# Loading every fourth streamed weight piece with two transfers, of 120 and of 8 partitions

## The chip, the cores and the metric

The kernel runs on one core of one Trainium2 chip. The metric is the device time of one execution in microseconds (us); lower is better. Where two kernels are compared, the ratio is the mean time of the fast runs of one kernel over the mean time of the fast runs of the other in the same rounds, so it is not quite the ratio of the medians that are quoted.

## The reference, cut to what matters

A recurrent attention over 64 segments of 32 tokens, with 8 memory tokens that each segment hands to the next, is mixed by a gate with a gated feed-forward network of the same input.

```python
mem = mem0
for s in range(n_seg):                       # 64, one after the other: mem is the carry
    h = concatenate([mem, x[:, 32*s:32*s+32]])
    q = einsum('btd,dhe->bhte', h, Wq)       # Dm = 640, H = 32, Dh = 192
    k = einsum('btd,dhe->bhte', h, Wk)
    v = einsum('btd,dhe->bhte', h, Wv)
    p = softmax(where(mask, q @ k.T * scale, -1e9))
    o = einsum('bhte,hed->btd', p @ v, Wo)
    mem = o[:, :8]
    outs.append(o[:, 8:])
a = concatenate(outs)
b = (gelu(x @ w_gate) * (x @ w_up)) @ w_down
return g * a + (1 - g) * b                   # g = sigmoid(sum(x * gate_w))
```

The four attention weights are needed again in each of the 64 segments. They don't all fit into on-chip memory, so a part is resident and the rest is streamed anew for each segment.

## The kernel before

The weights are cut into pieces. A piece of Wq, Wk or Wv is 128 partitions of 3,072 bytes (384 KB); a piece of Wo is 128 partitions of two rows of 1,280 bytes (320 KB). In each segment 24 pieces are streamed, 15 of the first kind and 9 of the second, through a ring of five slots. SyncE issues the loads. Before each it waits until PE has used up the piece that had the slot.

```python
B_RING = int(opts.get("ring", 5))
r_ring = [sreg(o, GQ) for o in ring_off]
...
def piece_src(key):
    if key[0] == 3:
        return Wo2[:, 2 * key[1]:2 * key[1] + 2, :]
    m, o_, k = key
    return (Wq2, Wk2, Wv2)[m][:, k, OW * o_:OW * (o_ + 1)]
...
def issue_ring(seg, upto):
    done = issued.get(seg, 0)
    while done <= upto:
        key = order[stream_list[done]]
        slot = stream_counter[0] % B_RING
        S_.add("sp", lambda e, slot=slot, key=key: e.dma_start(piece_view(key, ring_off[slot]), piece_src(key)),
               writes=[r_ring[slot]], dma_sem="ring%d" % slot, name="ring s%d p%d" % (seg, done))
        stream_counter[0] += 1
        ring_of[(seg, key)] = slot
        done += 1
    issued[seg] = done
```

Per four segments, `perm_dma` loads 128 rows of x, loads 128 rows of the feed-forward result and stores 128 rows of output, each as two transfers whose memory side is a view of four groups of rows:

```python
def rows(ap, g):
    v = ap[128 * g:128 * g + 128, :].rearrange("(s t) d -> s t d", t=L)
    return v[:, 0:XA, :], v[:, XA:L, :]      # four times 24 rows, four times 8 rows
```

## Time and profile before

| what | number | from |
|---|---|---|
| time | 2167.59 us median of 3 (2164.26 to 2174.91) | runs |
| loop of 64 segments | from about 330 us on, 28.6 us each | trace |
| PE busy in the loop | 85% | windows |
| DMA in the loop | 96% busy, 322 GB/s | windows |
| PE waiting for the four weights | 158 us | waits |
| median 3,072-byte packet | 121 ns (mean 141) | packets |

The page's own view of the transfers: busy tenths and rate in 40 slices of the span, then packets by queue.

```profile
DMA  9203579999999999999999999999999999999998
GB/s 366 103 13 89 149 220 341 328 321 337 322 325 316 310 326 329 313 327 311 329 328 314 324 315 332 323 307 316 334 319 333 320 325 306 328 327 328 322 321 273
...
q1 hardware_dynamic: 311914, 601.41, 81.6%
...
q8 instruction: 315, 5.16, 0.9%
```

From slice 7 on, the last slice apart, the sixteen DMA engines are busy at least 90% of the time. Queue 1 is SyncE's, with the weights. Queue 8 holds 315 packets of 16 KB. PE has two times 40,326 = 80,652 instructions, which is 315 blocks of 256 to within one block, so these are PE's instruction fetches.

The chain of work that ended last, by engine and by line:

```profile
DMA 48%; PE 37%; DVE 9%; ACTq 3%; issue 2%; ACT 2%; SPq 0%; POOL 0%; DVEq 0%; POOLq 0%
DMA arena<-in_A_Wq_dram 19%; DMA arena<-in_A_Wo_dram 13%; DMA arena<-in_A_Wv_dram 10%; PE ps L872 9%; PE ps L1021 7%; PE ps L899 5%; DMA arena<-in_A_Wk_dram 4%; PE ps L804 3%; PE ps L742 2%; ACTq L819 2%; PE ps L739 2%; PE ps L757 2%; PE ps L992 2%; DVE arena L975 2%; DVE arena L1008 1%
```

Waits of PE, longest in total first (us, times, longest one), and the issues of the ring (count, KB, median us from issue to landing):

```profile
PE ps L872 <- DMA arena<-in_A_Wq_dram: 77.6, 127, 1.9
...
PE ps L899 <- DMA arena<-in_A_Wv_dram: 32.2, 50, 1.8
PE ps L1021 <- DMA arena<-in_A_Wo_dram: 30.6, 63, 3.0
...
PE ps L872 <- DMA arena<-in_A_Wk_dram: 12.3, 16, 1.5
```

```profile
arena<-in_A_Wo_dram SPq DMA_DIRECT2D x591, 320.0 KB, 4.9
arena<-in_A_Wq_dram SPq DMA_DIRECT2D x404, 384.0 KB, 5.3
arena<-in_A_Wv_dram SPq DMA_DIRECT2D x335, 384.0 KB, 5.1
```

And the middle of the loop, from 600 to 1800 us (window, its length, busy us and instructions of PE, PE's weight loads, DVE, ACT, POOL, then granted clock, DMA share, GB/s):

```profile
600.00:1800.00 1200.00, 1016.72 (x25314) 668.11 (x25318) 747.97 (x2482) 353.79 (x885) 174.56 (x773) 0.98 0.96 322
```

Half of the chain is flights of weight pieces, and PE's largest waits are for them. So what makes a piece land earlier or later is worth time here.

### The profile page before, as it was taken

How to read it: one execution, taken by the hardware profiler on the slowest of the kernel's cores; microseconds unless marked ns; L12 is line 12 of the kernel's file. 1: busy time of each engine (PE TensorE's matmuls, PEld its weight loads, DVE VectorE, ACT ScalarE, POOL GpSimd, SP SyncE). 2: the span in 40 equal slices, each digit the busy share in tenths (PEclk: the TensorE clock that was granted, in tenths of full speed). 3: DMA queues.
4: the chain of work that ended last, by engine and by line, in shares of the span. 5: the costliest groups of instructions: out<-in, count | busy, mean ns of one | idle time of the engine just before them, and what ended most of it. 6: DMA issues, size and time to landing. Idle time of an engine off the chain costs nothing.

```text
span 2166.5 us, 92005 instructions
## 1 busy us (share of the span) xinstructions
PE 1836.7 (85%) x40326; PEld 1154.9 (53%) x40326; DVE 1231.5 (57%) x3952; ACT 618.8 (29%) x1480; POOL 274.1 (13%) x1210
## 2 busy tenths in 40 slices
PE   7999948888888888888888888888888888888887
PEld 3544425555555555555555555555555555555555
DVE  2222316666656566656666666656666666666665
ACT  2222212333232223332322223322323222323232
POOL 0000001111111111111111111111111111111111
PEclk9999979999999999999999999999999999999999
DMA  9203579999999999999999999999999999999998
GB/s 366 103 13 89 149 220 341 328 321 337 322 325 316 310 326 329 313 327 311 329 328 314 324 315 332 323 307 316 334 319 333 320 325 306 328 327 328 322 321 273
DMA packets 363391, 642.97 MB, mean 297 GB/s; under 512 B 60514, under 2 KB 231786, under 8 KB 362986
## 3 DMA queue, kind: packets, MB, share of 16 engines
q1 hardware_dynamic: 311914, 601.41, 81.6%
q10 hardware_dynamic: 51072, 35.66, 5.7%
q8 instruction: 315, 5.16, 0.9%
q14 instruction: 90, 0.74, 0.1%
HBM read 619.13 MB, written 17.83 MB: 294 GB/s over the span
## 4 chain that ended last, share of the span: by engine, by line
DMA 48%; PE 37%; DVE 9%; ACTq 3%; issue 2%; ACT 2%; SPq 0%; POOL 0%; DVEq 0%; POOLq 0%
DMA arena<-in_A_Wq_dram 19%; DMA arena<-in_A_Wo_dram 13%; DMA arena<-in_A_Wv_dram 10%; PE ps L872 9%; PE ps L1021 7%; PE ps L899 5%; DMA arena<-in_A_Wk_dram 4%; PE ps L804 3%; PE ps L742 2%; ACTq L819 2%; PE ps L739 2%; PE ps L757 2%; PE ps L992 2%; DVE arena L975 2%; DVE arena L1008 1%
## 5 line engine op out<-in xcount | busy, mean ns | idle before, releaser
L872 PE MATMUL ps<-arena 128*32 128x384 bf16 x10240 | 566.8, 331 | 119.9 <-DMA arena<-in_A_Wq_dram 77.6
L1021 PE MATMUL ps<-arena 128*128 128x40 bf16 x15360 | 472.1, 181 | 71.7 <-DVE arena L1008 35.9
L1021 PEld LDWEIGHTS ps<-arena 128*128 128x128 bf16 x15360 | 434.9, 97 | 116.8 <-DVE arena L1008 48.0
L872 PEld LDWEIGHTS ps<-arena 128*32 128x32 bf16 x10240 | 239.6, 96 | 346.5 <-DMA arena<-in_A_Wq_dram 172.1
L876 ACT ACTIVATE arena<-ps 128x384 bf16<-128x384 f32 x512 | 251.4, 491 | 552.2 <-PE ps L872 446.8
L899 PE MATMUL ps<-arena 128*32 128x384 bf16 x6400 | 333.1, 331 | 37.0 <-DMA arena<-in_A_Wv_dram 32.2
L835 POOL COPY arena<-arena 128x96 bf16<-128x96 bf16 x256 | 67.6, 264 | 1645.1 <-PE ps L931 1089.0
L899 PEld LDWEIGHTS ps<-arena 128*32 128x32 bf16 x6400 | 150.5, 97 | 175.6 <-DMA arena<-in_A_Wv_dram 82.0
L882 DVE STREAM_TRANSPOSE arena<-arena 128x384 bf16<-128x384 bf16 x256 | 146.0, 570 | 102.3 <-ACT arena L876 102.3
L975 DVE TENSOR_TENSOR arena<-ps,arena 128x320 bf16<-128x320 bf16 x256 | 125.8, 491 | 125.9 <-PE ps L973 121.9
L1002 ACT ACTIVATE arena<-ps 128x320 bf16<-128x320 f32 x256 | 110.7, 432 | 229.4 <-PE ps L994 229.4
L910 ACT ACTIVATE arena<-ps 128x384 bf16<-128x384 f32 x256 | 125.6, 491 | 161.9 <-PE ps L899 161.9
L839 POOL COPY arena<-arena 64x32 bf16<-64x32 bf16 (+1 forms) x768 | 165.7, 216 | 47.3
L959 DVE TENSOR_REDUCE arena<-ps 104x4 f32<-104x160 f32 x256 | 82.6, 323 | 150.6 <-ACT ps L957 148.6
L992 PE MATMUL ps<-arena 128*128 128x160 bf16 (+1 forms) x768 | 133.7, 264 | 39.6 <-DVE arena L978 38.0
L889 DVE STREAM_TRANSPOSE arena<-arena 64x128 bf16<-64x128 bf16 x512 | 145.5, 284 | 8.1
L957 ACT ACTIVATE ps<-ps 104x160 f32<-104x160 f32 x256 | 74.0, 289 | 233.9 <-DVE ps L947 189.0
L994 PE MATMUL ps<-arena 128*128 128x64 bf16 (+1 forms) x768 | 128.0, 206 | 2.1 <-DMA arena<-in_A_Wv_dram 1.0
L945 DVE TENSOR_REDUCE arena<-ps 104x4 f32<-104x160 f32 x256 | 81.0, 316 | 77.0 <-PE ps L931 77.0
L885 DVE STREAM_TRANSPOSE arena<-arena 128x256 bf16<-128x256 bf16 x256 | 111.4, 435 | 16.1 <-ACT arena L876 16.1
L992 PEld LDWEIGHTS ps<-arena 128*128 128x128 bf16 x768 | 73.9, 99 | 85.5 <-DVE arena L978 60.3
L1006 DVE CAST arena<-ps 64x160 bf16<-64x160 f32 x256 | 80.4, 314 | 52.5 <-PE ps L994 48.4
(79 smaller groups left out, 1719.8 us busy)
## 6 DMA issues: line engine op xcount, KB each, us to landing
arena<-in_A_Wo_dram SPq DMA_DIRECT2D x591, 320.0 KB, 4.9
arena<-in_A_Wq_dram SPq DMA_DIRECT2D x404, 384.0 KB, 5.3
arena<-in_A_Wv_dram SPq DMA_DIRECT2D x335, 384.0 KB, 5.1
arena<-in_A_Wk_dram SPq DMA_DIRECT2D x276, 384.0 KB, 5.3
left_qk_scratch<-arena ACTq DMA_DIRECT2D x16, 768.0 KB, 8.8
arena<-left_qk_scratch ACTq DMA_DIRECT2D x64, 192.0 KB, 4.5
arena<-in_A_x_dram SPq DMA_DIRECT2D x4, 640.0 KB, 15.1
ffn_b_scratch<-arena ACTq DMA_DIRECT2D x16, 160.0 KB, 1.8
```

The costliest lines, as they stand in the source:

```text
L839: S_.add("pool", lambda e, a=a, b=b, lo=lo, hi=hi, sa=sa: e.tensor_copy(out=Ks[lo:hi, a:b, L:R], in_=stg[lo:hi, o, 1, sa:sa + b - a]), rea ...
L872: S_.add("pe", [lambda e, j=j, k=k, gv=gv: e.matmul(ps[32 * j:32 * j + 32, bank, 0:384].rearrange("p (c i) -> p c i", i=32), Hb[hb][:, k, ...
L876: S_.add("act", lambda e: e.activation(out=rows_sb[m], in_=ps[:, bank, 0:384], func=ACTF.Copy), reads=[r_ps[bank]], writes=[r_rows[m]], na ...
L882: S_.add("dve", lambda e: e.transpose(out=Qs[:, :, 0:L], in_=rows_sb[0].rearrange("p (c r) -> p c r", r=L)), reads=[r_rows[0]], writes=[r_ ...
L885: S_.add("dve", lambda e: e.transpose(out=apx(Ks[:, 0, :], [[2 * R, 4], [R, 2], [1, L]]), in_=apx(rows_sb[1], [[96, 4], [64, 2], [1, L]])) ...
L889: S_.add("dve", lambda e, a=a, lo=lo: e.transpose(out=Ks[lo:lo + 64, a:a + 4, 0:L], in_=src[lo:lo + 64, :, 1]), reads=[r_rows[1]], writes= ...
L899: return [lambda e, j=j: e.matmul(ps[32 * j:32 * j + 32, bk, 0:384], lhs, g_[:, 384 * j:384 * (j + 1)], start=(k == 0), stop=(k == KT - 1) ...
L910: S_.add("act", lambda e: e.activation(out=v_sb[o % NVB], in_=ps[:, bank, 0:384], func=ACTF.Copy), reads=[r_ps[bank]], writes=[r_v[o % NVB ...
L975: S_.add("dve", lambda e: e.tensor_tensor(out=PTm, in0=apx(pv[:, 512:616], [[64, 2], [0, 4], [1, R]]), in1=apx(mbd, [[0, 2], [1, 4], [0, R]]),
L992: return [lambda e: e.matmul(full, v[:, e0:e0 + 128], PTm[:, ia:ib], start=True, stop=False, skip_group_check=True), lambda e: e.matmul(pa ...
L994: lambda e: e.matmul(part, vl[:, e0:e0 + 128], PTl[:, ia:ib], start=False, stop=True, skip_group_check=True)]
L1021: fns.append(lambda e, g_=g_, i=i, c=c, n=n, tl=tl, cc=cc, u=u: e.matmul(ps[:, OB, n * R:(n + 1) * R], g_[:, i, n * 128:(n + 1) * 128], u[ ...
```

## The change

The intent rests on an assumption: that a transfer of 120 partitions leaves out one of the DMA engines, the one that has extra work (here, the instruction fetches). Then a piece in four that passes it by could let it catch up. The eight partitions left over go in a small second transfer.

```diff
+    r_rings = [(sreg(o, GQ, 0, 120), sreg(o, GQ, 120, 128)) for o in ring_off]
...
-            S_.add("sp", lambda e, slot=slot, key=key: e.dma_start(piece_view(key, ring_off[slot]), piece_src(key)),
-                   writes=[r_ring[slot]], dma_sem="ring%d" % slot, name="ring s%d p%d" % (seg, done))
+            cut = 120 if done % 4 == 1 else 128
+            for lo, hi in ((0, cut), (cut, 128)):
+                if lo < hi:
+                    S_.add("sp", lambda e, slot=slot, key=key, lo=lo, hi=hi: e.dma_start(
+                        piece_view(key, ring_off[slot])[lo:hi], piece_src(key)[lo:hi]),
+                        writes=[r_ring[slot] if cut == 128 else r_rings[slot][lo > 0]], dma_sem="ring%d%s" % (slot, "t" if lo else ""),
+                        name="ring s%d p%d" % (seg, done))
```

## The prediction

> **What bounds the kernel now.** From about 330 us the kernel runs 64 segments of about 28.6 us. There the windows table gives PE 85% busy, DMA engines 96% and 322 GB/s; the chain of waits is 48% DMA, nearly all ring pieces (24 a segment: 15 of 384 KB, 9 of 320 KB), 37% PE. The waits view has PE idle about 157 us for the four weights.
>
> One DMA engine is the laggard. The sixteen semaphore landings of a ring transfer lie evenly, except the last: for 384 KB medians are 3.15 us (first), 4.59 (15th), 5.17 (16th) after issue. Queue 8 explains it: 315 packets of 16 KB, exactly 80,652 PE instructions in blocks of 256; they never overlap each other and take 0.96 us about every 6 us, 17% of one engine's time.[...] Estimate from packet times (121 ns per 3,072 B, 55 per 1,280 B): a segment costs each engine about 22.5 us, this one 27 of 28.6.
>
> **Which engine?** The trace does not number engines. [...]loads of 8 and 5 partitions and of 4-row views show 9, 6 and 5 semaphore writes[...].[...] I take it to be the last, at about 0.8.
>
> **What changes.** Pieces 1, 5, 9, 13, 17, 21 of each segment (four of 384 KB, two of 320 KB) go as 120 partitions[...] plus 8[...].[...] SyncE issues 6 more transfers a segment (0.33 to 0.40 us each; it mostly waits). PE waits on one more semaphore for these. Bytes and arithmetic stay.
>
> **Worth.** Had each 16th landing come with its 15th, 127 of 167 us of PE's ring waits would go, at first order; along the chain, 177 ring flights carry 146 us of that gap. Not all is had: the next engine is close, fetches still delay momentarily,[...] the tail is issued 0.35 us later, PE, once faster, asks sooner, and waits for DVE stay. I expect half: about 65 us (3%).
>
> **Predicted: 2105 us, 2050 to 2165 with 8 in 10.** Faster by over 2%: 0.60; within 2%: 0.31; slower: 0.09.
>
> **What would show it.** Right: the 16th landing within 0.3 us of the 15th, median landing 4.6 to 4.9 us; PE's waits for weights 60 to 110 us; loop bandwidth 330 to 340 GB/s at unchanged bytes; less DMA in the chain; queue 8 unchanged. Wrong on the engine: the last gap unchanged[...] or larger[...]. Wrong on size: gap gone but PE waits barely smaller.
>
> **What would make it wrong.** The fetch engine is not the last;[...] transfers run less evenly; the tail, queued behind other work, becomes the new last landing; SyncE's extra issues delay bursts.

The forecast came to about 65 us gained: half of the 127 to 146 us that the last landings cost by the trace, the half being a guess. Terms, namely what each engine gains and loses in a segment, rested on which engines a transfer uses, which no trace shows, and are not in the 65 us as numbers. "The last" engine is a name from that same assumption.

## The result, and the profile after

| | before | after |
|---|---|---|
| time, median of 4 | 2165.93 us (2161.73 to 2174.91) | 2461.09 us (2449.19 to 2476.15) |
| ratio of the fast runs | | 1.134, 95% interval 1.128 to 1.140 |

The prediction was 2105 us; the kernel became 13% slower instead. Each of the 384 cut pieces (6 x 64) costs (2461.09 - 2165.93) / 384 = 0.77 us.

The transfers of the changed kernel, by slices and queue:

```profile
DMA  9105699999999999999999999999999999999998
GB/s 371 43 23 136 185 283 270 279 278 283 281 273 276 283 271 280 273 289 276 276 272 280 279 279 281 267 280 276 293 277 283 277 292 279 268 278 284 279 274 239
...
q1 hardware_dynamic: 314602, 601.42, 85.6%
...
q8 instruction: 315, 5.16, 1.0%
```

Its chain by engine, PE's waits, and ring issues, as above:

```profile
DMA 64%; PE 27%; DVE 4%; ACTq 3%; issue 1%; ACT 1%; SPq 0%; POOL 0%; DVEq 0%
```

```profile
PE ps L878 <- DMA arena<-in_A_Wq_dram: 102.3, 179, 2.7
PE ps L878 <- DMA arena<-in_A_Wk_dram: 79.7, 149, 1.7
PE ps L1027 <- DMA arena<-in_A_Wo_dram: 79.2, 169, 2.0
PE ps L905 <- DMA arena<-in_A_Wv_dram: 63.1, 89, 2.6
PE ps L1000 <- DMA arena<-in_A_Wv_dram: 46.1, 79, 2.7
```

```profile
arena<-in_A_Wq_dram SPq DMA_DIRECT2D x404, 384.0 KB, 6.0
...
arena<-in_A_Wv_dram SPq DMA_DIRECT2D x192, 360.0 KB, 6.7
arena<-in_A_Wv_dram SPq DMA_DIRECT2D x143, 384.0 KB, 6.0
```

```profile
600.00:1800.00 1200.00, 933.70 (x21927) 598.54 (x21919) 650.41 (x2158) 307.56 (x768) 150.22 (x666) 0.96 0.99 278
```

Bytes and fetches are the same (601 MB, 315). The engines are busier than before (0.99) and move less: 278 GB/s against 322. An engine that is busy and moves less has slower packets, and that is what the packet records of the loop show (computed from the trace's packets of queue 1, from 330 to 2150 us):

| 3,072-byte packets in the loop | before | after |
|---|---|---|
| mean / median | 141 / 121 ns | 170 / 151 ns |
| share at the floor (at most 124 ns) | 87% | 31% |

The fetch packets became slower too (mean 1.01 to 1.19 us). PE's granted clock was a little lower (0.96 against 0.98) and its busy time longer (1836.7 to 1926.4 us), but its share of the chain fell from 37 to 27%, and the streams below are slow with PE idle, so this is not the main cause. The uncut pieces are hit as well: Wq is cut nowhere, yet its pieces land after 6.0 us instead of 5.3. So the question is not what the second transfer costs, but why most packets take longer, those of the uncut pieces too.

The semaphore writes: in the loop a 120-partition load shows 16, the first of them 0.54 us after the issue (median of 326 loads; the second at 3.72 us), and its tail shows 9, as the one load of 8 partitions in the kernel before. In an uncut 384 KB piece of the kernel before the first of the 16 comes after 3.15 us. How many engines that makes, no trace shows.

### The profile page after: what moved, and what is told of

Same layout as the page of the kernel before. It is cut to its first block, busy times and chain, and to the rows that moved or that the text cites. A ratio compares the mean times of both kernels' runs of the same rounds, so it can differ in the third digit from the quotient of the medians.

```text
span 2457.5 us, 92505 instructions
## 1 busy us (share of the span) xinstructions
PE 1926.4 (78%) x40298; PEld 1189.3 (48%) x40326; DVE 1232.7 (50%) x3952; ACT 620.0 (25%) x1480; POOL 273.6 (11%) x1210
## 4 chain that ended last, share of the span: by engine, by line
DMA 64%; PE 27%; DVE 4%; ACTq 3%; issue 1%; ACT 1%; SPq 0%; POOL 0%; DVEq 0%
DMA arena<-in_A_Wo_dram 21%; DMA arena<-in_A_Wq_dram 17%; DMA arena<-in_A_Wv_dram 15%; DMA arena<-in_A_Wk_dram 10%; PE ps L1027 5%; PE ps L878 5%; PE ps L905 5%; PE ps L810 3%; PE ps L748 2%; ACTq L825 2%; PE ps L745 2%; PE ps L763 2%; DVE arena L981 1%; PE ps L998 1%; DMA arena<-in_B_w_up_dram 1%
## 5 line engine op out<-in xcount | busy, mean ns | idle before, releaser
L878 PE MATMUL ps<-arena 128*32 128x384 bf16 x10240 | 614.9, 338 | 206.1 <-DMA arena<-in_A_Wq_dram 102.3
L1027 PE MATMUL ps<-arena 128*128 128x40 bf16 x15360 | 496.8, 182 | 111.2 <-DMA arena<-in_A_Wo_dram 79.2
L1027 PEld LDWEIGHTS ps<-arena 128*128 128x128 bf16 x15360 | 449.6, 98 | 167.5 <-DMA arena<-in_A_Wo_dram 104.2
L878 PEld LDWEIGHTS ps<-arena 128*32 128x32 bf16 x10240 | 243.3, 97 | 466.5 <-DMA arena<-in_A_Wq_dram 193.6
L905 PE MATMUL ps<-arena 128*32 128x384 bf16 x6400 | 349.7, 334 | 78.7 <-DMA arena<-in_A_Wv_dram 63.1
L905 PEld LDWEIGHTS ps<-arena 128*32 128x32 bf16 x6400 | 167.2, 97 | 211.3 <-DMA arena<-in_A_Wv_dram 107.2
L1000 PE MATMUL ps<-arena 128*128 128x64 bf16 (+1 forms) x768 | 133.2, 209 | 47.8 <-DMA arena<-in_A_Wv_dram 46.1
L998 PEld LDWEIGHTS ps<-arena 128*128 128x128 bf16 x768 | 75.2, 101 | 74.7 <-DVE arena L984 41.8
L1000 PEld LDWEIGHTS ps<-arena 128*128 128x128 bf16 x768 | 76.9, 100 | 68.6 <-DMA arena<-in_A_Wv_dram 68.0
```

The source lines that it names most:

```text
L878: S_.add("pe", [lambda e, j=j, k=k, gv=gv: e.matmul(ps[32 * j:32 * j + 32, bank, 0:384].rearrange("p (c i) -> p c i", i=32), Hb[hb][:, k, ...
L905: return [lambda e, j=j: e.matmul(ps[32 * j:32 * j + 32, bk, 0:384], lhs, g_[:, 384 * j:384 * (j + 1)], start=(k == 0), stop=(k == KT - 1) ...
L998: return [lambda e: e.matmul(full, v[:, e0:e0 + 128], PTm[:, ia:ib], start=True, stop=False, skip_group_check=True), lambda e: e.matmul(pa ...
L1000: lambda e: e.matmul(part, vl[:, e0:e0 + 128], PTl[:, ia:ib], start=False, stop=True, skip_group_check=True)]
L1027: fns.append(lambda e, g_=g_, i=i, c=c, n=n, tl=tl, cc=cc, u=u: e.matmul(ps[:, OB, n * R:(n + 1) * R], g_[:, i, n * 128:(n + 1) * 128], u[ ...
```

## The experiments

My theory formed after the result: packets take longer because of where a transfer of another shape writes, and the number of partitions tells which shapes are slow. The grounds that I gave for it, in terms of engines and of the memory they write, no trace shows. Where a text names no theory, the first numbers are those that this one led me to expect.

The rivals: the second transfer and its semaphore; unequal work of the engines; the tail of eight partitions; the order in which memory rows are read.

Where only a number at the end of a kernel was wanted, loads were added after the last output; they don't touch the result.

### Lone loads

```diff
     out_store(NG - 1)
+    r_mic = sreg(0, ring_bytes)
+    def lone(n, dst, src):
+        for rep in range(3):                 # each waits for the one before: same region
+            S_.add("sp", lambda e: dst(e, src), writes=[r_mic], dma_sem="mic%d" % n, watch=True)
+    lone(0, lambda e, s: e.dma_start(sb(slice(0, 128)), s), hb(0, 128))    # Wq rows, 4 x 3,072 bytes each
+    lone(1, lambda e, s: e.dma_start(sb(slice(0, 120)), s), hb(0, 120))
     ...
+    lone(5, lambda e, s: e.dma_start(sb(slice(120, 128)), s), hb(120, 128))
+    lone(7, lambda e, s: e.dma_start(sb(slice(0, 32, 4)), s), hb(120, 128))
```

> The kernel before, with 42 lone loads at its very end (14 shapes, three times each, each issued after the one before has landed; rows of 3,072 bytes, four per partition). [...]a packet takes about 121 ns in the 128-partition load, but about twice that (230 to 250 ns) in the loads of 120, 112, 64 and 60 partitions and of 32[...], and about four times (450 to 490 ns) in 8 partitions in[...]; back to about 121 ns[...] for 8 partitions in steps of four[...]. Rival, transfer count and engine balance (each transfer costs a fixed time, the packets don't care where they go): about 121 ns in all of them, times set by packets per engine alone. Rival, memory side (rows read in a bad order): the 8 rows with destinations in steps of four stay as slow as the 8 rows to neighbours. The kernel itself unchanged, longer only by the loads at the end (some 150 to 250 us).

(The loads "in a row" went to the eight neighbouring partitions 120 to 127.) After that I put the pattern into a rule, before the second set. No trace shows what it counts, and it had to set the load of 128 partitions apart.

> Lone loads at the end again, twelve other shapes, three times each. The first lone loads (120: 241 ns a packet, 64: 234, 60: 236, 112: 175, against 121 in 128)[...]. The rule therefore expects a median packet of 121 ns for 128, 126, 117 and 117 from partition 2, about 240 for 120, 230 to 245 or (as 112) 175 to 240 for 105, 104 and 96, 240 to 360 for 45. 15 partitions in steps of nine: from first packet to landing 1.0 to 1.4 us; 15 neighbours, the same rows: about 1 us longer. The rival,[...] a number of partitions that is not a multiple of 16 is slow as such[...]: 126 and 117 stretched like 120.

Measured in both (packets of 3,072 bytes, three loads of each shape; the whole of it at a time when nothing else ran):

| partitions | median packet, ns | landing after issue, us |
|---|---|---|
| 128 | 121 | 6.4 to 6.8 |
| 126 | 121 | 6.9 to 7.3 |
| 117 | 121 | 6.7 to 7.6 |
| 120 | 239 to 245 | 9.6 to 10.0 |
| 104 | 239 to 244 | 9.4 to 9.5 |
| 64 | 230 to 235 | 6.0 to 6.3 |
| 60 | 235 to 237 | 5.9 to 6.2 |
| 96 | 195 to 208 | 7.4 to 7.5 |
| 112 | 172 to 182 | 7.3 to 7.5 |
| 105 | 145 to 167 | 6.7 to 7.3 |
| 45 | 271 to 303 | 5.8 to 5.9 |
| 32 | 130 to 151 (mean 212 to 215) | 3.9 to 4.1 |

Issues of the second set on SyncE's queue (start, time from the first of three issues to the end of the third, line, count). L1095 is 128 partitions, L1096 126, L1097 120, L1098 117, L1101 104:

```profile
2167.99 13.61 SPq L1095 DMA_DIRECT2D arena<-in_A_Wq_dram  x3
2188.08 14.67 SPq L1096 DMA_DIRECT2D arena<-in_A_Wq_dram  x3
2209.32 20.01 SPq L1097 DMA_DIRECT2D arena<-in_A_Wq_dram  x3
2238.58 13.83 SPq L1098 DMA_DIRECT2D arena<-in_A_Wq_dram  x3
...
2301.54 19.26 SPq L1101 DMA_DIRECT2D arena<-in_A_Wq_dram  x3
```

Each of these times holds two landings and one issue. 120 partitions take about 1.4 times as long as 126 (20.01 against 14.67 us), although they are fewer. A 120-partition load alone has packets of about twice the floor (239 to 245 against 121 ns). A number that isn't a multiple of 16 is not slow as such: 126 and 117 stay at the floor (121 ns), while 112, 96 and 64 don't (172 to 235 ns). The rule's expectation for the second set told the fast shapes (126 and 117) from the slow ones (120, 105, 104, 96, 45), with 105 less slow than expected (145 to 167 against 175 to 245 ns). Why these shapes differ is not shown.

Two pairs that read the same rows into other partitions speak against the memory side. Time from the first packet to the landing: rows 120 to 127 into eight neighbouring partitions, 2.2 to 2.3 us; the same rows into partitions 0, 4, ... 28, 1.1 to 1.2 us. Fifteen rows into neighbours, 2.4 us; the same into partitions 0, 9, ... 126, 1.3 to 1.4 us. From issue to landing they differ by less (3.1 to 3.2 against 2.6 to 2.7, and 3.3 to 3.4 against 2.9 to 3.1), because the first packet of the stepped loads comes later (1.5 to 1.7 us after the issue against about 0.9, by difference). There the packets themselves end early in either case (median 121 to 123 ns), and into neighbours the landing comes 1.0 to 1.3 us after the last packet's end, against 0.3. Why is not shown. For the large shapes the memory side was not tested by a pair of its own. My expectation of 450 ns for these packets was wrong, and so was that of 230 to 250 ns for 32 partitions. Three shapes of the first set missed their aim: memory views of 8 or 2 groups were to change the engines in use, but the semaphore writes (16 and 9) are as many as without them, so those three say nothing.

### Two transfers, but of columns

```diff
+            cut = done % 4 == 1
+            for n in range(2 if cut else 1):
                 ... half(piece_view(key, ring_off[slot]), key, n) ... half(piece_src(key), key, n)
```

> The same pieces in two transfers, but cut along the columns: both halves have 128 partitions[...]. [...]within 2% of the kernel before (2165 us), packets at their floor. Rival, two transfers and a second semaphore cost the time: slower by several per cent, up to the 13% of the change.

Measured: 2197.51 us against 2169.59, ratio 1.014 (1.009 to 1.019). 3,072-byte packets stay at a mean of 141 ns. So as many second transfers, issues and semaphores as in the change, all of 128 partitions, cost 1.4%; the smaller packets of the halved rows may be part of it (not separated). The middle of the loop stays near that of the kernel before:

```profile
600.00:1800.00 1200.00, 1013.99 (x25111) 665.40 (x25113) 746.79 (x2479) 352.65 (x881) 174.47 (x768) 0.99 0.95 319
```

### The same pieces as 112 and 16 partitions

```diff
+            parts = [(0, 112), (112, 128)] if done % 4 == 1 else [(0, 128)]
```

> The same pieces cut into 112 and 16 partitions[...]. [...]clearly slower, by 7 to 15%, with stretched packets (mean of 3,072-byte packets 155 to 175 ns against 141). Rival, engine balance[...]: as before within 2%.

Measured: 2388.58 us, ratio 1.102 (1.097 to 1.106); mean packet 164 ns (141 before). I took every engine to have as many packets here as before; no trace shows that, so this speaks against unequal work as the main cause only if it holds. The middle of the loop:

```profile
600.00:1800.00 1200.00, 961.37 (x22704) 617.41 (x22704) 674.78 (x2237) 317.23 (x793) 157.04 (x691) 0.96 0.99 288
```

### Main part without the tail

```diff
+            parts = [(0, 120)] if done % 4 == 1 else [(0, 128)]     # 120..127 keep an older piece: wrong on purpose
```

> Only the 120-partition part of the cut pieces is loaded, the last 8 partitions keep an older piece (a wrong result on purpose). It tells main part from tail. If the main part is the cost: still 7 to 13% slower than before. If the tail[...] is the cost: near the time before or faster, 2080 to 2170 us[...]. If both: between, 4 to 8% slower.

Measured: 2416.01 us, ratio 1.114 (1.109 to 1.118), result wrong. So about 11 of the 13% come with the large part, and about two with the tail (roughly, since this kernel also moves 1.5% fewer weight bytes, 592 MB).

### 126 and 2 partitions

Alone, the packets of 126 partitions were as short as those of 128. If what makes a lone load slow were the whole story, this cut would repair the change. (The rival here: any cut along the partitions is slow.)

```diff
+            parts = [(0, 126), (126, 128)] if done % 4 == 1 else [(0, 128)]     # and with done % 8 == 1
```

> The change with another cut: 126 and 2 partitions instead of 120 and 8, every fourth piece. [...]most of the loss goes: 2110 to 2230 us, at most 3% slower than before and at least 9% faster than the change; if relieving the fetch engine is worth what was predicted, up to 3% faster than before. Rival[...]: 10% or more slower than before.

> The same with every eighth piece cut (three in a segment). [...]between before and every fourth, 2110 to 2200 us[...]. Rival: 5% or more slower.

Measured: every fourth piece, 2436.56 us, ratio 1.124 (1.120 to 1.127), mean packet 166 ns; every eighth, 2274.81 us, ratio 1.052 (1.046 to 1.058). Both expectations were missed, the first by 9% even from its upper end (2230 us): the theory was not complete. The middle of the loop with 126 and 2 looks like that of the change:

```profile
600.00:1800.00 1200.00, 938.61 (x22117) 602.86 (x22117) 658.64 (x2182) 310.50 (x774) 152.52 (x672) 0.95 0.98 280
```

### The change at a third of the dose

```diff
+            parts = [(0, 120), (120, 128)] if done % 12 == 5 else [(0, 128)]
```

> The change itself (120 and 8) at a third of the dose: two pieces in a segment. If each cut piece costs the same (0.76 us, 292 us over 384 cut pieces), 3.5 to 6% slower than before, 2245 to 2295 us. If a few cut pieces suffice[...], nearly as slow as the change. If relief pays at a small dose, within 2%.

Measured: 2265.27 us, ratio 1.045 (1.041 to 1.049): (2265.27 - 2164.64) / 128 = 0.79 us for each cut piece, as in the full change. For this cut the cost is proportional to the number of cut pieces at the two doses tried, and no gain shows at the small one. For 126 and 2 it is less so: 0.71 us for each cut piece at every fourth, 0.57 at every eighth.

### Streams, as in the ring

What differs between a lone load and the loop is that other pieces are in flight. So pieces of one shape, and of two shapes mixed, were sent as in the ring, without the loop.

```diff
+    def stream(n, parts):
+        for j in range(20):                  # five slots in flight
+            P = parts[j % len(parts)]
+            S_.add("sp", lambda e, j=j, P=P: e.dma_start(arena[0:P, (j % 5) * OW:(j % 5 + 1) * OW], Wq2[0:P, j % KT, 0:OW]),
+                   writes=[r_ring[j % 5]], dma_sem="mic%d_%d" % (n, j % 5), watch=True)
+    stream(0, [128]); stream(1, [126]); stream(2, [128, 126]); stream(3, [120])
+    stream(4, [128, 120]); stream(5, [128, 128, 128, 120]); stream(6, [128, 128, 128, 126]); stream(7, [128])
```

> The kernel before with eight streams of 20 ring loads at its end (3,072 bytes a partition, five in flight, as in the loop): all 128 partitions; all 126; 128 and 126 by turns; all 120; 128 and 120 by turns; three of 128 and one of 120; three of 128 and one of 126; all 128 again. The cut of 126 was as slow in the loop as that of 120, though alone it was not. Theory A[...]. Expected: all 128: packets 121 ns in median, 300 to 340 GB/s; all 126 between; 128 and 126 by turns stretched (mean over 155 ns, rate at least 8% under all 128), three to one less so, 120 slowest (180 to 220 GB/s). Theory B (126 is slow in the loop only for the tail of two partitions or for the loop's waits): the streams of 126 and the mixed ones at the floor like 128.

The eight streams in this order, each from its first issue to its last landing; the last two numbers are DMA share and GB/s (the first stream overlaps the end of the kernel):

```profile
2161.40:2185.30 23.90, 0.45 (x5) 0.28 (x5) 1.61 (x4) 0.00 (x0) 0.00 (x0) 0.54 0.91 336
2188.50:2217.60 29.10, 0.00 (x0) 0.00 (x0) 0.00 (x0) 0.00 (x0) 0.00 (x0) 0.50 0.84 266
2220.70:2251.30 30.60, 0.00 (x0) 0.00 (x0) 0.00 (x0) 0.00 (x0) 0.00 (x0) 0.50 0.90 255
2254.50:2286.40 31.90, 0.00 (x0) 0.00 (x0) 0.00 (x0) 0.00 (x0) 0.00 (x0) 0.50 0.90 231
2289.70:2318.90 29.20, 0.00 (x0) 0.00 (x0) 0.00 (x0) 0.00 (x0) 0.00 (x0) 0.50 0.91 261
2322.20:2351.20 29.00, 0.00 (x0) 0.00 (x0) 0.00 (x0) 0.00 (x0) 0.00 (x0) 0.50 0.86 267
2354.40:2383.00 28.60, 0.00 (x0) 0.00 (x0) 0.00 (x0) 0.00 (x0) 0.00 (x0) 0.50 0.88 274
2386.30:2408.90 22.60, 0.00 (x0) 0.00 (x0) 0.00 (x0) 0.00 (x0) 0.00 (x0) 0.50 0.93 348
```

All 128: 336 and 348 GB/s, 86 to 95% of packets at the floor. All 126: 266 GB/s, 4% at the floor, though alone their median packet was at it (121 ns). One cut piece in four, with 120 or with 126: 267 and 274 GB/s, 36 and 37% at the floor. That is the loop of the changed kernel (278 GB/s, 31%) without PE, segments or waits, and with no tail. With PE idle here, no consumer can be the cause. A cause on the memory side (the order in which engines read rows when several pieces are in flight) was not tested in a stream.

### 126 without its tail

```diff
+            parts = [(0, 126)] if done % 4 == 1 else [(0, 128)]     # 126 and 127 keep an older piece: wrong on purpose
```

> 126 of 128 partitions loaded for every fourth piece, the last two left with older data (a wrong result on purpose): no tail, no second transfer, fewer bytes. Theory A: still 9 to 12.5% slower than before. Theory B (the tail of two partitions[...], or the second transfer and its semaphore): within 3% of before.

Measured: 2422.26 us, ratio 1.114 (1.106 to 1.122). Its output is wrong, which doesn't matter for the time. The loss of the 126 cut is in its large part too.

### Row loads as transfers of 128 partitions

The loop of the kernel before has transfers of another shape too: its row loads and stores, with five semaphore writes each against 16 of a weight piece ("four-engine transfers" in the text, a name that rests on those five writes). In this kernel x and the feed-forward result are put into their permuted order once, before the loop, so that a row load is one transfer of 128 partitions.

```diff
-  perm_dma(lambda j: rowb[PP[j]], lambda j: rows(x2, g + 1)[j], [], r_rowbh, "rowb")     # and the same for b_scr
+  S_.add("act", lambda e: e.dma_start(rowb, x_prm[128 * g:128 * g + 128, :]), ...)       # x_prm, b_prm made before the loop
```

> An attempt to beat the kernel before[...]: in the loop the kernel before already has transfers[...], the row loads of x and of the other branch's result (96 and 32 partitions, twice per four segments). Here both are put into their permuted order once, memory to memory, before the loop, so that each row load is one transfer of 128 partitions[...]. In the trace of before, ring pieces in flight beside a four-engine transfer land 0.9 us later than others (5.8 against 5.0 us), and segments without one take 27.7 us against 28.5 to 29.5. Expected: correct, 2105 to 2150 us (1 to 3% faster). If the four-engine transfers cost nothing that matters: within 0.5% of before, or slower by the copies.

Measured: correct, 2161.56 us against 2165.82, ratio 0.997 (0.992 to 1.002). That is the same time. By their place in a group of four (cut at the copies of L1068 and L1088, profiles of one execution each, first group left out), the two segments with a row load got shorter (28.7 to 28.3 us and 29.3 to 28.6), the one with neither load nor store and the one with the output store got a little longer (27.7 to 27.9 and 29.1 to 29.4; why is open). Over the loop that leaves a gain of 7 us, but the loop starts 10 us later (first such copy at 363.6 against 353.1 us), with the two permutations made before it. The expected 1 to 3% is not there. I have no version that beats the kernel before.

### Which engine carries the fetches?

The last question is the premise. The premise was tested directly: PE runs small matmuls, so that fetches keep coming, beside lone loads of 15, 12, 8 and 4 partitions in steps of nine. Which engines such a load uses no trace shows; that a load of 15 leaves out the engine that the prediction calls the last is taken over from the prediction.

```diff
+    for n in range(12):
+        S_.add("pe", [lambda e: e.matmul(ps[:, 0, 0:8], ident, ident[:, 0:8], start=True, stop=True)] * 640, ...)
+    def few(c):
+        probe(c, arena[0:9 * (c - 1) + 1:9, 0:4 * OW].rearrange("p (k n) -> p k n", n=OW), Wq2[0:c, 0:4, 0:OW])
+    for rep in range(12):
+        probe(16, arena[:, 0:OW], Wq2[:, 0, 0:OW]); few(15); few(12); few(8); few(4)
```

> Tests the premise that the engine of PE's instruction fetches is the last of the sixteen. At the end of the kernel before, PE runs 7,680 small matmuls (15,360 instructions, some 60 fetches of 16 KB) while SyncE sends lone loads: 128 partitions[...], and 15, 12, 8 and 4 partitions in steps of nine[...]. Where a fetch falls into a load that uses its engine, the last landing comes late by up to 1 us after the one before it; elsewhere never. If the fetch engine is the last: late last landings only in the 128 loads (a quarter to a half of the twelve), none in the loads of 15, 12, 8, 4.[...]

The loads of the second run have five rows a partition, 40 rounds of 15, 12, 8 and 4, and 30 instead of 12 blocks of matmuls (some 150 fetches):

> As fetch_probe, with 160 lone loads of 15, 12, 8 and 4[...].[...] If each class has its own engine, every class is consistent in itself: late last landings (gap over 250 ns) in nearly all well-placed loads that use its engine, none in the smaller ones, and the classes fall at different engines.[...] If instead the classes mix (the same class delays a load of eight once and does not another time),[...] the place of the fetches stays open. If nearly all classes spare the loads of 15, the premise of the prediction was right after all.

A load counts as met if a fetch runs through its data phase (from at latest 250 ns to at least 400 ns after the first packet); it counts as late if its last landing comes over 250 ns after the one before. Of 57 loads with no fetch within 250 ns of their packets, none was late.

| late of met | 4 partitions | 8 | 12 | 15 | 128 |
|---|---|---|---|---|---|
| first run | 0 of 3 | 2 of 8 | 3 of 5 | 1 of 1 | 2 of 3 |
| second run | 0 of 16 | 3 of 15 | 10 of 12 | 14 of 14 | |

If one engine carried all fetches and the loads of 15 left it out, none of those would be late. In the second run all 14 were. If one engine carried them all, and loads of one shape used the same engines each time (not shown), each column would be all or nothing; those of 8 (3 of 15) and 12 (10 of 12) are not. One load of the 128 column of the first run (192 ns) is just under the limit. What decides which loads a fetch delays these counts don't show, so for the loop of the kernel before the share of each engine stays open. (The classes in the expectation of the second run sort the fetches by their order. I have no count for each class here. That each has its own engine was a supposition to be tested; no trace names an engine.)

## Why the prediction was wrong, point by point

- **What bounds the loop**: held. Flights of weight pieces are half of the chain, and when they got slower the kernel followed: the DMA share of the chain rose from 48 to 64%, and PE's waits for Wq, Wk, Wo and Wv from 158 to 384 us (102.3 + 79.7 + 79.2 + 63.1 + 46.1, with 13.4 more in a smaller line).
- **"One DMA engine is the laggard"**: this step failed where it was tested, in the probes. In the second one 27 of 57 loads met by a fetch had one landing late (by 0.4 to 1.4 us), but of the loads of 8 and 12 partitions only some (3 of 15 and 10 of 12), which one engine would not do if loads of one shape use the same engines each time (not shown). One landing of sixteen is late, and I read "one of sixteen" as "the same one". In the loop before, fetches explain only a part of it: counted from issue to last landing, the last landing of a ring transfer comes 0.27 us after the one before it in the mean of the 130 transfers that no fetch touches, and 0.53 us in the other 1391. The prediction's own test came out against it as well: in the uncut 384 KB pieces the last gap stayed (mean 0.54 us before, 0.55 after), and the median landing went from 5.17 to 6.17 us instead of 4.6 to 4.9.
- **"Which engine?"**: the guess of the last, at 0.8, failed with it. Of the loads of 15 partitions, which by the prediction's own reading spare the last, 14 of 14 were delayed by a fetch in the second probe.
- **"What changes"**: bytes (601 MB), number of transfers and fetches (315) came as said. This is the step that turned the expected gain into a loss: missing was the one term that mattered, how long packets take when some transfers have another shape. I took a packet of the cut pieces to last about as long as before; alone it takes 239 to 245 ns, and in the loop packets of all pieces went from 141 to 170 ns in the mean.
- **"Worth", about 65 us gained**: 295 us were lost. About 11% of the 13 come with the large part, shown by leaving the tail out; the rest, about two, with tail and second transfer. A second transfer that keeps all 128 partitions cost 1.4% (interval 0.9 to 1.9).
- **"What would make it wrong"** did name transfers that run less evenly, but gave it no cost.
- **Shown and not shown.** Shown by lone loads: some shapes slow the packets up to twofold (2.5 for 45 partitions), others not at all (126 and 117), and the partition count alone doesn't explain which. Shown by two pairs with the same rows: the partitions they are written to change the time to the landing (2.2 to 2.3 against 1.1 to 1.2 us). Shown by the streams: one transfer in four of another shape slows the whole ring (267 and 274 GB/s against 336 and 348), whether that shape is slow alone (120) or not (126). Not shown: why. The trace does not name engines, and what my theory said of them is not more than a guess. Open: whether relieving an engine could pay. Neither 120 nor 126 partitions kept the packets at the floor in a stream; I tried no other shape there.

## What to carry to other kernels

Keep a bandwidth-bound stream in transfers of all 128 partitions, and cut along the columns if a cut is needed: 1.4% here, where cuts along the partitions cost 10 to 13%. A shape must be tested in a stream with its neighbours in flight; the packets of 126 partitions were at the floor alone, and in the ring this cut cost 12%, nearly as much as 120. When one of many parallel completions is always the late one, check that it is always the same engine before relieving one.
